# Operand pieces of the last layer in fixed slots, three queue orders changed, and the tail's splits one tile ahead

## The chip, the cores and the metric

The kernel runs on one core of a Trainium2 chip. The metric is the device time of one launch, in microseconds (us), as the median of several runs. TensorE (PE in the profile; PEld is its weight load) multiplies matrices into PSUM banks, VectorE (DVE) and ScalarE (ACT) work on tiles in SBUF and PSUM, GpSimd (POOL) works on SBUF tiles and issues indirect DMAs, and SyncE (SP) issues the other DMAs. Each engine takes its own instructions in program order and waits for semaphores of the others.

## The reference, cut to what matters

```python
x = attention(q, k, v)            # sliding window of 64, 4 x 8 heads, 576 positions of 64
x = moe(x, ...)                   # 2304 tokens, 8 experts, the best two of each token
g   = x @ w_gate                  # last layer: 2304 x 512 by 512 x 1536
val = x @ w_val                   # the same shape
out = (g * 1 / (1 + exp(-g)) * val) @ w_out     # 2304 x 1536 by 1536 x 512
```

All of it is float32. The change touches the last layer (`_moe2_ref`) and the end of the expert layer that feeds it.

## The kernel before, in words

**Precision.** A matrix operand is cut into two parts, hi and lo (`x = hi + lo`). ACT copies hi into an fp32r tile, DVE subtracts it from the original to get lo, and three products (hi-hi, hi-lo, lo-hi) are accumulated. So each operand costs one ACT copy and one DVE subtraction before TensorE may use it.

**The two wide products.** `g` and `val` are computed together as one 2x2 block product with seven block products instead of eight (Strassen-Winograd). Its operands are seven blocks of x (IA11, IA12, IS1 to IS4, IA22) and seven of the weights (IB11, IB21, IT1 to IT4, IB22); the S and T blocks are sums, made by DVE in place in the raw tile. `x_pieces(p)` makes the x blocks of one third p of the tokens (six tiles of 128), `w_pieces(k)` the weight blocks of one slice k of 128 columns. Raw weights are loaded by `load_w(k)` into one tile, `wr`, through SP's queue.

**A unit** is one pair (slice, third): seven block products of six 128x384 matmuls each (L1049). There are 36, in the order of the list `units`. `unit(n)` writes the program of unit n interleaved with the end of unit n-1: `first`, `second`, IS4 of n-1, IS2, IS3, IA22 of n-1, IS1. The products IA11, IS2, IS1 (and IS4 one unit later) go one after another into the same bank B. Between them `keep` copies the bank's running sum out on ACT (L1059); the next product into that bank must wait for that copy. `add` (L1066) adds bank A or D to a kept sum on DVE, `gate` takes the sigmoid on ACT (L1070), `times` multiplies on DVE or POOL (L1073), `store` writes the result u to DRAM through SP. The tile S1 of the kept sum has one buffer, S2 and S4 have two.

**The queue of pieces.** Everything that is not part of a unit (splits, sums, loads, gathers, combining of expert outputs) stands in a list `todo2`. `other()` pops one entry; it is called seven times in a unit and five times in a product of the third kind. The list `plan` says at which unit which entries are appended; an entry then gets whatever call comes next.

**The third product.** `third(T)` multiplies tile T of u (128 tokens) by w_out: 36 matmuls of 128x512 (L1176). `load_u(T)` reads the tile back, `u_pieces(T)` splits it in two halves (L1161 on ACT, L1162 on DVE) into one of two buffers. From unit 26 on one `third` follows each unit; the eight tiles 10 to 17 come after the last unit, back to back. They are "the tail" below. The result of each tile is copied from its bank to one buffer, by ACT for even and DVE for odd tiles, and scattered to its rows by POOL.

**Before the first unit** the last expert's five second products (`mm2`, L278) run. Between them `last_mm2(t)` gathers the expert outputs of the tokens (`early_y`, POOL), weighs them (`weigh`: ACT L729, DVE L730), transposes them on TensorE (`trans_c`, L195, copied out by ACT L742), and starts the x and w pieces.

Of the kernel before, what the change touches and what calls it, by code (L numbers as in the profile page):

```python
# [53 lines left out]
def tile_attention_moe_swiglu(ctx: ExitStack, tc: tile.TileContext, qh, kh, vh, wgn, noise, w1h, w2h,  # L54
# [655 lines left out]

    def other(k=1):
        for _ in range(k):
            if todo2:
                todo2.pop(0)()
# [29 lines left out]
    def x_pieces(p):  # L744
# [11 lines left out]
        def start():  # L756
            XS2[p] = pools[f"x{p}"].tile([128, 2, 7, 2, NB2], F32R, name=f"x{p}", tag=f"x{p}")
            hi(IA11, 0)
            sm(4, 2, ALU.add, 3)

        return [start,
                lambda: (hi(IA12, 1), lo(IA11, 0)),
                lambda: (hi(IS1, 4), lo(IA12, 1), sm(2, 0, ALU.subtract, 2)),
                lambda: (hi(IS3, 2), lo(IS1, 4), sm(4, 4, ALU.subtract, 0)),
                lambda: (hi(IS2, 4), lo(IS3, 2)),
                lambda: (hi(IA22, 3), lo(IS2, 4), sm(4, 1, ALU.subtract, 4)),
# [5 lines left out]
    def load_w(k):  # L772
        WR[k] = w = pools["rw"].tile([128, 7, 2, 128], F32, name=f"wr{k}", tag="wr")
# [4 lines left out]
    def w_pieces(k):  # L778
        def sums():
            WS2[k] = pools["rw" if k % 3 < 2 else "x2"].tile([128, 2, 7, 2, 128], F32R, name=f"ws{k}",  # L780
                                                             tag=f"ws{k % 3}")
            w = WR[k]
            for o, a, b in ((IT1, IT3, IB11), (IT2, IB22, IT1), (IT3, IB22, IT3), (IT4, IB21, IT2)):
                nc.vector.tensor_tensor(w[:, o], w[:, a], w[:, b], op=ALU.subtract)  # L784
# [118 lines left out]
    if True:  # L903
# [24 lines left out]
        def last_mm1(f):  # L928
# [6 lines left out]
            if f == 7:  # L935
# [6 lines left out]
                todo2.extend(x_pieces(0))  # L942

        def last_mm2(t):
            if t == 0:
                nc.scalar.preload_act_table_set("sigmoid_and_others")
                other(5)
            if t == 1:
                other(3)
                scopes["p2"].close()  # L950
                pools["x1"] = pool("x1", "right")
                weigh(6)
                weigh(7)
            if t == 2:
                trans_c(6)
                trans_c(7)
                weigh(8)
                todo2.extend(w_pieces(0))
                other(3)
                load_w(1)  # L960
                early_y(9)
                early_y(10)
            if t == 3:
                trans_c(8)
                early_y(11)
                weigh(9)
                weigh(10)
            if t == 4:
                trans_c(9)
                trans_c(10)  # L970
                weigh(11)
# [61 lines left out]
    for fs in ((0, 1, 2), (3,), (4,), (5,), (6,), (7,), (8,), (9,), (10, 11)):  # L1033
# [47 lines left out]
    def unit(n):  # L1081

        now, old = n < NU, n > 0
# [6 lines left out]
        other()  # L1090
        if now:
            second(n)
            add(n, A_[n], S1)
        other()
        if old:
            prod(B_[m], m, IS4, IB22, False, True)
        if now:
            gate(n, 0, S1)
        if old:
            times(m, 0, B_[m])  # L1100
            store(m, 0)
        other()
# [4 lines left out]
        other()  # L1107
# [3 lines left out]
        other()  # L1111
# [3 lines left out]
        other()  # L1115
# [3 lines left out]
        if old:  # L1119
            gate(m, 1, S2)  # L1120
            times(m, 1, S2[m])
            times(m, 1, S4[m], nc.gpsimd if now else nc.vector)
            store(m, 1)
        other()
# [4 lines left out]

    def o_load(j):  # L1130
        if j == 0:
            OW["a"] = pools["x0"].tile([128, 2, 10, 512], F32R, name="ow", tag="x0")
            r = rx.tile([128, 3584], F32, name="ur", tag="xr")
# [225 lines left out]
```

## Time and profile before

| | us |
|---|---|
| median of 3 runs | 1055.04 (1054.79 to 1057.38) |
| the profiled execution's own time | 1062.48 |
| its span, first to last instruction | 1060.7 |
| TensorE busy | 991.2 (93%) |
| VectorE busy | 683.8 (64%) |
| ScalarE busy | 432.3 (41%) |
| GpSimd busy | 227.3 (21%) |

The profiled execution lies 7.4 us above the median; 1.8 us of its time lie outside the span. Busy times are summed over a core's whole span, over stages that are limited by different things, so the stages have to be looked at one by one.

### The profile page before, as it was taken

What the parts mean: (1) busy time and instruction counts of PE and PEld (TensorE: products, weight loads), DVE (VectorE), ACT (ScalarE), POOL (GpSimd) and SP (SyncE); (2) the same over time, 40 slices, a digit from 0 to 9 for tenths busy, and PEclk for the clock granted to TensorE, in tenths of its full rate; (3) what the DMA queues carried; (4) which work ended last, traced back from release to release, by engine and by line L of the source; (5) the groups of instructions that cost most, each with busy time, mean ns of one, the idle gap of its engine ahead of it and who ended that gap; (6) DMA issues with size and microseconds to landing.
All of it is one profiled execution on the core that took longest, in us unless ns stands there. A gap on an engine that the chain in (4) does not pass through costs nothing.

```text
span 1060.7 us, 17386 instructions
## 1 busy us (share of the span) xinstructions
PE 991.2 (93%) x6538; PEld 875.5 (83%) x6538; DVE 683.8 (64%) x1318; ACT 432.3 (41%) x952; POOL 227.3 (21%) x301
## 2 busy tenths in 40 slices
PE   7978999999999999999999897899998999999886
PEld 5756888889898898989897797889997889988664
DVE  5797836868786877878256666687667665653211
ACT  6867334414242333324255543554445333432210
POOL 2693025123111010010053051011124111111100
PEclk9989999999999999999999998999999999999999
DMA  7884136657685767666254254223356334443320
GB/s 227 293 266 121 38 118 211 198 192 219 187 242 184 222 189 220 201 202 210 71 148 149 88 145 130 59 66 86 99 150 177 112 119 142 139 121 110 104 96 32
DMA packets 115009, 161.31 MB, mean 152 GB/s; under 512 B 15383, under 2 KB 77975, under 8 KB 114919
## 3 DMA queue, kind: packets, MB, share of 16 engines
q1 hardware_dynamic: 101799, 126.79, 39.6%
q0 software_dynamic: 7936, 23.91, 7.5%
q10 hardware_dynamic: 5184, 9.44, 2.4%
q8 instruction: 53, 0.87, 0.3%
q14 instruction: 37, 0.30, 0.1%
HBM read 117.07 MB, written 43.04 MB: 151 GB/s over the span
## 4 chain that ended last, share of the span: by engine, by line
PE 68%; DVE 14%; issue 6%; DMA 5%; ACT 5%; SPq 0%; ACTq 0%; POOL 0%; DVEq 0%
PE y L278 19%; PE h L256 16%; PE o L1176 13%; PE b L1049 8%; PE d L1049 4%; DVE wr L784 2%; PE a L1049 2%; DMA wr<-w_d 2%; PE sc L419 1%; PE gt L236 1%; ACT ws L787 1%; DVE s L1066 1%; ACT u L1070 1%; DMA k<-in_k_dram 1%; DVE nm L429 1%
## 5 line engine op out<-in xcount | busy, mean ns | idle before, releaser
L278 PE MATMUL y<-wp,ht 128*128 128x512 f32 (+6 forms) x960 | 228.7, 394 | 0.0
L256 PE MATMUL h<-xh,wp 128*128 128x256 f32 (+6 forms) x1536 | 221.5, 304 | 4.1 <-DVE ht L261 2.7
L256 PEld LDWEIGHTS h<-xh,wp 128*128 128x128 f32 x1536 | 215.7, 189 | 8.4 <-DVE ht L261 5.0
L278 PEld LDWEIGHTS y<-wp,ht 128*128 128x128 f32 (+6 forms) x960 | 172.5, 183 | 40.6
L1049 PE MATMUL b<-x,ws 128*128 128x384 f32 x864 | 171.4, 345 | 18.4 <-ACT s L1059 18.2
L1049 PEld LDWEIGHTS b<-x,ws 128*128 128x128 f32 x864 | 154.5, 192 | 25.3 <-ACT s L1059 24.5
L1176 PE MATMUL o<-ow,ou 128*128 128x512 f32 x540 | 129.7, 395 | 11.9 <-DVE ou L1162 6.2
L1176 PEld LDWEIGHTS o<-ow,ou 128*128 128x128 f32 x540 | 101.8, 190 | 36.5 <-DVE ou L1162 8.8
L221 POOL DMA_INDIRECT xg<-x_d,idx_i x38 | 36.8, 967 | 287.7 <-PE gt L236 241.2
L258 ACT ACTIVATE ht<-h 128x256 fp32r<-128x256 f32 (+7 forms) x128 | 53.1, 422 | 108.0 <-PE h L256 87.3
L1059 ACT ACTIVATE s<-b 128x384 f32<-128x384 f32 x108 | 52.4, 485 | 92.3 <-PE b L1049 89.4
L1073 POOL TENSOR_TENSOR u<-s,u 128x384 f32<-128x384 f32 x35 | 37.1, 1061 | 241.3 <-DVE u L1073 204.3
L283 ACT ACTIVATE ys<-y 128x512 f32<-128x512 f32 (+6 forms) x40 | 23.8, 596 | 159.5 <-PE y L278 137.0
L1049 PE MATMUL d<-x,ws 128*128 128x384 f32 x432 | 81.9, 337 | 0.4 <-DVE s L1066 0.4
L127 DVE TENSOR_TENSOR wp<-raw,wp 128x1024 fp32r<-128x1024 f32 x55 | 67.4, 1226 | 21.7 <-ACT wp L126 16.2
L1049 PEld LDWEIGHTS d<-x,ws 128*128 128x128 f32 x432 | 75.6, 188 | 1.0 <-DVE s L1066 1.0
L261 DVE SCALAR_TENSOR_TENSOR ht<-h,ht 128x256 fp32r<-128x256 f32 (+7 forms) x128 | 59.3, 467 | 19.5 <-ACT ht L258 17.8
L241 DVE TENSOR_TENSOR xh<-gt,xh 128x512 fp32r<-128x512 f32 (+6 forms) x40 | 25.7, 662 | 68.7 <-ACT xh L238 62.4
L1162 DVE TENSOR_TENSOR ou<-ur,ou 128x768 fp32r<-128x768 f32 x36 | 33.6, 953 | 55.9 <-ACT ou L1161 55.9
L1073 DVE TENSOR_TENSOR u<-s,u 128x384 f32<-128x384 f32 x73 | 42.9, 588 | 40.2 <-ACT u L1070 40.0
L787 ACT ACTIVATE ws<-wr 128x1024 fp32r<-128x1024 f32 (+1 forms) x48 | 44.4, 945 | 59.2 <-DVE wr L784 59.2
L126 ACT ACTIVATE wp<-raw 128x1024 fp32r<-128x1024 f32 x55 | 58.1, 1056 | 17.0 <-DMA raw<-in_w_dram 12.7
(206 smaller groups left out, 1342.7 us busy)
## 6 DMA issues: line engine op xcount, KB each, us to landing
raw<-in_w_dram SPq DMA_DIRECT2D x64, 512.0 KB
u_d<-u SPq DMA_DIRECT2D x72, 192.0 KB
ur<-u_d SPq DMA_DIRECT2D x18, 768.0 KB
wr<-w_d SPq DMA_DIRECT2D x48, 256.0 KB
w_d<-da ACTq DMA_DIRECT2D x36, 256.0 KB
y_d<-ys SPq DMA_DIRECT2D x34, 256.0 KB
rd<-in_wg_dram SPq DMA_DIRECT2D x12, 512.0 KB
rd<-in_wv_dram SPq DMA_DIRECT2D x12, 512.0 KB
```

Source lines behind the costliest of these rows:

```text
L126: nc.scalar.activation(w[:, 0, :], r, AF.Copy)
L127: nc.vector.tensor_tensor(w[:, 1, :], r, w[:, 0, :].bitcast(F32), op=ALU.subtract)
L221: nc.gpsimd.indirect_dma_start(out=g[0:m, :], out_offset=None, in_=x_d[0:rows, :], in_offset=bass.IndirectOffsetOnAxis(ap=idx(t)[0:m, :], ...
L256: nc.tensor.matmul(b_, w[:, a, k, fc], xh[:, c, k, 0:m], start=(n == 0), stop=(n == 11))
L258: nc.scalar.activation(ht[:, 0, f, 0:m], b_, AF.Relu)
L261: nc.vector.scalar_tensor_tensor(ht[:, 1, f, 0:m], b_, 0.0, ht[:, 0, f, 0:m].bitcast(F32), op0=ALU.max, op1=ALU.subtract)
L278: nc.tensor.matmul(b_, ht[:, a, f, sl], w[:, c, f % 2, :], start=(f == 0 and n == 0), stop=(f == 7 and n == 2))
L787: nc.scalar.activation(WS2[k][:, 0, a:b], WR[k][:, a:b], AF.Copy)
L1049: nc.tensor.matmul(b_, w[:, a, wi, k, :], x[:, c, xi, k, :], start=(start and i == 0), stop=(stop and i == 5), skip_group_check=True)
L1059: nc.scalar.activation(to[n], B_[n], AF.Copy)
L1073: eng.tensor_tensor(UT[n, h], v, UT[n, h], op=ALU.mult)
L1176: nc.tensor.matmul(ob, u[:, a, f, :], w[:, c, :], start=(f == 0 and n == 0), stop=(f == 11 and n == 2))
```

## The change: what it does

1. `todo2` holds pairs (slot number, entry). `slot_()` replaces `other()` in the units and the third products: it runs the entries whose number has come, and counts on. The numbers are written out (`put`, `w_put`); the list `plan` is gone.
2. `x_pieces` has eleven entries instead of eight and `w_pieces` five instead of three: the ACT copy and the DVE subtraction of one block stand in different entries.
3. In `unit`, `gate(n, 0)` is queued on ACT behind `keep(n, 2)` instead of ahead of it. `times(n, 0, S1)` stands one product later. The multiplications and the store of the second half of unit m (`times(m, 1, ...)`, `store(m, 1)`) stand in unit m+2 instead of at the end of unit m+1.
4. Raw weights of slices 4 and 5 are loaded into the place of the raw x tile (`xw`), those of slice 13 into a part of the tile for w_out.
5. At the end of the expert layer: the table load of the sigmoid set stands before the last expert's second products instead of behind the first of them; the gathers of tiles 9 to 11 get a tile of their own and stand behind the second of these products; the transposes of tiles 9 to 11 all stand behind the fourth; x pieces of the second third and the pieces of slice 1 stand there too.
6. In the list of units the slices 9, 10 and 11 form one group instead of (9) and (10, 11).
7. The splits of w_out are spread over units 22 to 26; two of the six subtractions are on POOL instead of four. `load_u(T + 2)` is issued at the end of the split of tile T. In the tail the split of tile T+1 stands inside `third(T)`.

```diff
     def other(k=1):
         for _ in range(k):
             if todo2:
-                todo2.pop(0)()
+                todo2.pop(0)[1]()
+    def slot_():
+        while todo2 and todo2[0][0] <= now_[0]:
+            other()
+        now_[0] += 1
...
-        def split(a, b):
+        def hi(a, b):
             nc.scalar.activation(WS2[k][:, 0, a:b], WR[k][:, a:b], AF.Copy)
+        def lo(a, b):
             nc.vector.tensor_tensor(WS2[k][:, 1, a:b], WR[k][:, a:b], WS2[k][:, 0, a:b].bitcast(F32), op=ALU.subtract)
-        return [sums, lambda: split(0, 4), lambda: split(4, 7)]
+        return [lambda: sums((IT1, IT3, IB11), (IT2, IB22, IT1)),
+                lambda: sums((IT3, IB22, IT3), (IT4, IB21, IT2)),
+                lambda: (place(), hi(0, 4)),
+                lambda: (hi(4, 7), lo(0, 4)),
+                lambda: lo(4, 7)]
...
             if t == 1:
...
+                for T in range(9, 12):
+                    early_y(T)
...
             if t == 3:
+                for T in range(9, 12):
+                    trans_c(T)
+                xq[:], wq = x_pieces(1), w_pieces(1)
+                todo2.extend((-1, o) for o in xq[:5] + wq[:2] + xq[5:6] + wq[2:])
...
+        if n > 1:
+            times(n - 2, 1, S2[n - 2])
+            times(n - 2, 1, S4[n - 2], nc.gpsimd if now else nc.vector)
+            store(n - 2, 1)
...
             prod(B_[m], m, IS4, IB22, False, True)
-        if now:
-            gate(n, 0, S1)
...
             prod(B_[n], n, IS2, IT2, False, False)
             keep(n, 2, S2)
-            times(n, 0, S1[n])
+            gate(n, 0, S1)
...
             if b == 12:
                 ready.add(("t", T))
+                if T < NT - 2:
+                    load_u(T + 2)
...
-        plan[last[k - 3] + 2] += w_pieces(k) + [lambda k=k: k + 1 < 24 and load_w(k + 1)]
+    put(2, (2,), [lambda: (w_raw(4), w_raw(5))])
+    w_put(5, 6, (4, 6, 7, 9, 10))
+        w_put(k, 2 * k - 4, (3, 4, 6, 7, 10), k + 1)
...
+    for T in range(12, NT):
+        todo2.extend((at(37, 5 * (T - 12) + s), o) for s, o in zip((0, 2), u_pieces(T)))
...
     for T in range(NU + 1 - 26, NT):
         third(T)
-        if T + 2 < NT:
-            load_u(T + 2)
-        if T + 1 < NT:
-            todo2.extend(u_pieces(T + 1))
```

The first place is ScalarE's queue in unit 7. `s_7` from `b` are the copies `keep`, `u_0` and `u_1` the sigmoids, `ws` the hi copies of a weight slice (slice 5 here). Before:

```order
474 L1059 ACTIVATE s_7_7207<-b_7200 128x384
475 L787 ACTIVATE ws_7210<-wr_7177 128x1024
476 L1070 ACTIVATE u_0_7231<-s_7_7207 128x384
477 L787 ACTIVATE ws_7210<-wr_7177 128x768
478 L1059 ACTIVATE s_7_7243<-b_7200 128x384
```

After, with the same names (`gl` is a gathered tile that is weighed):

```order
470 L1085 ACTIVATE s_7_7211<-b_7204 128x384
471 L801 ACTIVATE ws_7214<-xw 128x1024
472 L801 ACTIVATE ws_7214<-xw 128x768
473 L1085 ACTIVATE s_7_7243<-b_7204 128x384
474 L1096 ACTIVATE u_0_7245<-s_7_7211 128x384
475 L738 ACTIVATE gl<-gl,recp 128x512
```

The second copy of bank b stands ahead of the sigmoid now, and the weights come from the tile `xw`.

The second place is SP's queue of DMAs around the loads of slices 4 and 5 (from `w_d_81` and `w_d_82`); `u_d` are the stores. Before the change the queue reads:

```order
300 L1078 DMA u_d<-u_1_7117 128x3x128
301 L1078 DMA u_d<-u_0_7075 128x3x128
302 L776 DMA wr_7177<-w_d_81 128x4x128
303 L776 DMA wr_7177<-w_d_82 128x4x128
304 L1078 DMA u_d<-u_1_7195 128x3x128
```

After the change the same loads stand further ahead in the program (behind unit 1's first store):

```order
291 L1104 DMA u_d<-u_0_6805 128x3x128
292 L788 DMA xw<-w_d_81 128x4x128
293 L788 DMA xw<-w_d_82 128x4x128
294 L788 DMA xw<-w_d_81 128x4x128
295 L788 DMA xw<-w_d_82 128x4x128
296 L1104 DMA u_d<-u_1_6913 128x3x128
```

Before, slice 5 was loaded behind the store of the second half of unit 4 and the first half of unit 5; now slices 4 and 5 stand together, ahead of the store of unit 1's second half.

The third place is ScalarE's queue where the tail begins. `ur<-o` is the copy of an even tile's result, `ou` two to four halves of splits. Before:

```order
693 L1161 ACTIVATE ou<-ur 128x768 x2
694 L1070 ACTIVATE u_1_9842<-s_35_9751 128x384
695 L1181 ACTIVATE ur<-o_9847 128x512
696 L1161 ACTIVATE ou<-ur 128x768 x4
697 L1181 ACTIVATE ur<-o_9937 128x512
```

After the change the queue reads, from the split of tile 10 on:

```order
700 L1193 ACTIVATE ou<-ur 128x768 x2
701 L1096 ACTIVATE u_1_9842<-s_35_9746 128x384
702 L1193 ACTIVATE ou<-ur 128x768 x2
703 L1215 ACTIVATE ur<-o_9847 128x512
704 L1193 ACTIVATE ou<-ur 128x768 x4
705 L1215 ACTIVATE ur<-o_9937 128x512
```

Two more halves (the split of tile 11) stand ahead of the copy of tile 10's result.

## Rows read from the trace of the kernel before

**Rows 1.** The page's first part: busy us (share of the span) xinstructions.

```profile
PE 991.2 (93%) x6538; PEld 875.5 (83%) x6538; DVE 683.8 (64%) x1318; ACT 432.3 (41%) x952; POOL 227.3 (21%) x301
```

**Rows 2.** TensorE's waits from 589 to 821.4: us in total, times, longest.

```profile
PE b L1049 <- ACT s L1059: 18.2, 16, 4.1
PE ct L195 <- DVE gl L730: 3.2, 4, 1.6
```

**Rows 3.** TensorE's waits from 554 to 589.1.

```profile
PE ct L195 <- DVE gm L730: 2.2, 1, 2.2
PE ct L195 <- issue: 2.0, 1, 2.0
```

**Rows 4.** TensorE's waits from 969 to the end.

```profile
PE o L1176 <- DVE ou L1162: 6.2, 7, 1.4
PE o L1176 <- ACT ou L1161: 5.7, 4, 1.4
```

**Rows 5.** Windows by stage: length, busy us (x) of each engine, PEclk, DMA.

```profile
589.00:614.10 25.10, 22.00 (x111) 20.07 (x109) 21.20 (x32) 14.60 (x24) 3.91 (x3) 0.93 0.23 61
614.10:821.40 207.30, 188.61 (x1039) 182.38 (x1040) 144.98 (x241) 96.03 (x171) 45.71 (x39) 0.98 0.41 115
821.40:971.40 150.00, 149.80 (x751) 135.40 (x750) 86.91 (x135) 55.55 (x90) 21.53 (x31) 1.00 0.40 122
971.40:1053.80 82.40, 70.45 (x289) 54.52 (x288) 17.16 (x22) 13.16 (x19) 8.70 (x13) 0.98 0.27 88
```

**Rows 6.** Timeline of PE: the second product of units 3 and 5.

```profile
616.35 1.20 PE L1049 MATMUL a<-x,ws 128*128 128x384 f32 x6
...
630.98 1.22 PE L1049 MATMUL a<-x,ws 128*128 128x384 f32 x6
```

**Rows 7.** Pieces of the chain that ended last: start us, us, what.

```profile
821.48 8.16 PE o L1176 x36
...
975.17 4.77 DMA ur<-u_d
```

**Rows 8.** Timeline of all engines in unit 7: start, us, engine [idle before <-releaser].

```profile
646.85 2.52 SPq L776 DMA_DIRECT2D wr<-w_d  x2
...
652.49 1.56 DVE L784 TENSOR_TENSOR wr<-wr 128x256 f32<-128x256 f32 x4 [3.58 <-DMA wr<-w_d]
...
655.86 0.47 ACT L1059 ACTIVATE s<-b 128x384 f32<-128x384 f32 x1
...
656.38 1.01 PE L1049 MATMUL b<-x,ws 128*128 128x384 f32 x2 [4.15 <-ACT s L1059]
```

**Rows 9.** Window just behind that wait, columns as in rows 5.

```profile
656.30:662.00 5.70, 5.62 (x18) 5.34 (x18) 3.24 (x7) 2.03 (x5) 1.01 (x1) 0.56 0.44 127
```

**Rows 10.** Groups by form, DVE and ACT, from 589 to 980: busy, mean ns.

```profile
L1066 DVE TENSOR_TENSOR s<-d,s 128x384 f32<-128x384 f32 x72 | 39.7, 551 | 19.8 <-PE d L1049 19.6
L788 DVE TENSOR_TENSOR ws<-wr,ws 128x1024 fp32r<-128x1024 f32 x23 | 28.2, 1225 | 11.3 <-ACT ws L787 11.3
L788 DVE TENSOR_TENSOR ws<-wr,ws 128x768 fp32r<-128x768 f32 x23 | 21.8, 950 | 0.2 <-ACT ws L787 0.2
L747 ACT ACTIVATE x<-xr 128x768 fp32r<-128x768 f32 x14 | 11.4, 839 | 7.6 <-DVE xr L754 7.5
L787 ACT ACTIVATE ws<-wr 128x1024 fp32r<-128x1024 f32 x23 | 24.4, 1061 | 57.3 <-DVE wr L784 57.3
```

**Rows 11.** Timelines of ACT and POOL before the first unit.

```profile
559.92 0.60 ACT L283 ACTIVATE ys<-y 128x512 f32<-128x512 f32 x1 [4.89 <-issue]
560.53 1.28 ACT L946 ACT_TABLE_LOAD   x1
...
573.67 0.94 POOL L724 DMA_INDIRECT gm<-y_d,slot_e  x1 [11.83 <-PE ct L195]
```

**Rows 12.** Timelines of POOL and DVE in unit 23.

```profile
787.71 2.49 POOL L1147 TENSOR_TENSOR ow<-ur,ow 128x1024 fp32r<-128x1024 f32 x1 [0.87 <-ACT ow L1146]
...
789.00 1.61 DVE L1073 TENSOR_TENSOR u<-s,u 128x384 f32<-128x384 f32 x1
```

More of the change, by code (lines that the diff above doesn't have):

```diff
@@ L1081, in unit @@
     def unit(n):
-        now, old = n < NU, n > 0
+        now, old = n < NU, 0 < n <= NU
         m = n - 1
@@ L1105, in unit @@
             keep(n, 2, S2)
-            times(n, 0, S1[n])
-        other()
+            gate(n, 0, S1)
+        slot_()
         if now:
@@ L1110, in unit @@
             prod(D_[n], n, IS3, IT3, True, False)
-        other()
+        slot_()
+        if now:
+            times(n, 0, S1[n])
         if old:
@@ L1114, in unit @@
             add(m, D_[m], S2)
-        other()
+        slot_()
         if now:
@@ L1177, in third @@
             if f in (1, 3, 5, 7, 9):
-                other()
+                slot_()
         ot = OW["o"]
@@ L1224, in tile_attention_moe_swiglu @@
-    tiles = iter(range(NT))
-    def tile_next():
-        T = next(tiles)
-        need(("t", T))
-        third(T)
-        if T + 2 < NT:
-            load_u(T + 2)
-        if T + 1 < NT:
-            todo2.extend(u_pieces(T + 1))
-    for n in range(NU + 1):
-        if n <= 26:
-            todo2 += plan[n]
-        unit(n)
-        if n >= 26:
-            todo2 += wq if n == 26 else plan[n]
-            tile_next()
-    for T in range(NU + 1 - 26, NT):
-        todo2[:0] = [nothing]
-        tile_next()
@@ L1245, in tile_attention_moe_swiglu, with at, put, w_put @@
-    while todo2:
-        other()
+    def at(n, slot):
+        return 7 * min(n, 26) + 12 * max(n - 26, 0) + slot
+    def put(n, slots, pieces):
+        assert len(slots) == len(pieces)
+        todo2.extend((at(n, s), o) for s, o in zip(slots, pieces))
+    def w_put(k, n, slots, nxt=None, place=None):
+        ps = w_pieces(k)
+        if nxt:
+            last_ = ps.pop()
+            ps.append(lambda: (last_(), load_w(nxt, place and place())))
+        put(n, slots, ps)
+    raw = {}
+    def w_raw(k):
+        if not raw:
+            raw[0] = rx.tile([128, 3840], F32, name="xw", tag="xr")
+        load_w(k, raw[0][:, 1792 * (k - 4):1792 * (k - 3)])
@@ new lines, in tile_attention_moe_swiglu @@
+    put(0, (0, 3), xq[0:2])
+    w_put(2, 0, (4, 6, 7, 10, 11), 3)
+    put(1, (0, 6, 8), xq[2:5])
+    put(2, (2,), [lambda: (w_raw(4), w_raw(5))])
+    for T in range(12, 18):
+        put(T - 11, (5,), [lambda T=T: late_y(T)])
+    w_put(3, 4, (3, 4, 6, 7, 10), 6)
+    w_put(4, 5, (4, 6, 7, 9, 10))
+    w_put(5, 6, (4, 6, 7, 9, 10))
+    for k in range(6, 11):
+        w_put(k, 2 * k - 4, (3, 4, 6, 7, 10), k + 1)
+    w_put(11, 18, (3, 4, 6, 7, 10), 12)
+    for T, a, b in ((12, (7, 4), (8, 0)), (13, (7, 6), (8, 2)), (14, (9, 2), (9, 6)), (15, (9, 4), (10, 0)),
+                    (16, (10, 0), (11, 0)), (17, (10, 2), (11, 2))):
+        put(a[0], a[1:], [lambda T=T: weigh(T)])
+        put(b[0], b[1:], [lambda T=T: trans_c(T)])
@@ new lines, in tile_attention_moe_swiglu @@
+    for n in range(26, 36):
+        put(n, (2, 4), u_pieces(n - 26))
+        if n < 35:
+            w_put(n - 11, n, (7, 8, 9, 10, 11), n - 10 if n < 34 else None)
+    put(36, (2, 4, 7, 9), u_pieces(10) + u_pieces(11))
+    for T in range(12, NT):
+        todo2.extend((at(37, 5 * (T - 12) + s), o) for s, o in zip((0, 2), u_pieces(T)))
+    todo2.sort(key=lambda o: o[0])
+    for n in range(NU + 2):
+        unit(n)
+        if n == NU:
+            unit(n + 1)
+            third(n - 26)
+            break
+        if n >= 26:
+            third(n - 26)
@@ L1247, in tile_attention_moe_swiglu @@
+    for T in range(NU + 1 - 26, NT):
+        third(T)
+    assert not todo2
     for name in ("x2", "rs", "x1", "rw", "x0", "rx"):
```

151 lines of the change are left out of this document (72 added, 79 removed).

## Prediction

> **What bounds the kernel now.** I read the page first: TensorE is busy 93% of the span, the next engine 64% [rows 1]. So TensorE sets the time, and the question is where its time is more than its work. Then its waits by stretch, its timeline for the pace without waits, and a window for each stage. What to see: the pace of a unit is (630.98 - 616.35) / 2 = 7.32 us, or 1.045 for one of its seven products [rows 6], and a third product takes 8.16 [rows 7]. Against these, the stages stand so:
>
> - Before the first unit (554 to 589): waits of 2.2 and 2.0 [rows 3].
> - Units 0 to 2 (589.0 to 614.1): 18 products are 18.8 us of work in 25.1, so 6.3 are lost; 3.1 of it are idle (25.1 - 22.0), the rest is slow pace at a clock of 0.93 [rows 5].
> - Units 3 to 26 (614.1 to 821.4): 24 units and one product, 176.7, and six transposed tiles, put by estimate at a third of a product each, 2; so 28.6 of the 207.3 are lost, 18.7 idle [rows 5].
> - Units 27 to 36 with a third product each: TensorE is busy 149.8 of 150.0 [rows 5]. Nothing to win.
> - The tail: 8 x 8.16 = 65.3 of work in 82.4, so 17.1 are lost; its waits are 6.2 and 5.7 [rows 4, 5].
>
> In the second and third stages nearly all waits are for the copy of bank B (18.2 of 21.4, sixteen of them [rows 2]). Unit 7 shows how one comes about [rows 8]. SP issues the raw weights at 646.85 and DVE, which waits for them 3.58 us, starts the sums only at 652.49. Behind the sums on DVE stands the addition to S1, behind that addition on ACT the sigmoid, and behind the sigmoid the copy of bank B, which starts at 655.86. TensorE stood idle 4.15 us, though neither sums nor sigmoid concern its next product. After such a wait the granted clock is 0.56, near the lower of its two levels (1.2 GHz), for some microseconds: 18 matmuls took 5.7 us, at the pace above 3.1 [rows 9]. The long waits thus cost about half as much again as they show.
>
> **The change, part by part.** The sum is made against the profiled execution: 1062.48 us, of which 1060.7 are span. It lies 7.4 above the median, and the trace does not show where those come from; I take the saving off the median unchanged, and the upper end of the range allows for some of the 7.4 lying in waits that go away.
>
> Before the first unit. The table load (1.28) moves into ACT's idle 4.89, ahead of the first y copy [rows 11], so the x pieces start earlier; nothing waits for it, and without that cover it would cost its 1.28. The gathers of tiles 9 to 11, which waited 11.83 us on POOL for a transposed tile to leave its place [rows 11], now wait for the second y product only. The last transpose stands ahead of the fifth y product, which covers its copy. I keep about 1 us: three transposes share two banks, so the third of them waits for an ACT copy, twice. Saving 4.2 - 1.0 = 3.2; bounds 1 and 4.2.
>
> Units 0 to 2. ACT now gets four copies of pieces between the fifth y copy and the first `keep`: two of x at 0.84, one of w at 1.06, one of the 768 width, 0.84 by the x row [rows 10]. With the y copy's 0.60 [rows 11] that is 4.2 us, and the third product of unit 0 wants its copy 2 x 1.045 = 2.1 after the start: a wait of 2.1, plus about 0.5 for the copy itself. The raw weights of slice 2 share one tile with slice 1 and are asked for only behind its last split, and the multiplication that frees S1 (one buffer) is queued behind their sums on DVE: about 1 more. So 3.6 of the 6.3 remain: saving 2.7, say 2.5; bounds 0 (these waits also lower the clock, as now) and 5.
>
> Units 3 to 26. (a) The copy ahead of the sigmoid cuts the chain of unit 7 at its last link; nothing on TensorE waits for a sigmoid soon. (b) Slices 4 and 5 are in place three units before use; the 3.58 goes. (c) Later slices are loaded one unit, 7.32, before their sums; the load of unit 7 took 652.49 - 646.85 = 5.64 from issue to use [rows 8], so 1.7 us to spare. If one comes late, DVE's sums hold up the sigmoid of the second half and the weights' own copies, and the next unit's first copy behind those. (d) DVE in a unit with a slice: six of its own operations at 0.55, four sums 1.56, two subtractions 1.23 and 0.95 [rows 8, 10]: 7.0 of 7.32. It fits, with nothing to spare; but DVE need not keep time with each product, only stay within a few products. Over the stage DVE has 145 us of work [rows 5] for about 181. (e) The second half's multiplications stand a unit later; `keep` of the next sum into the same S2 buffer now waits for one of them. DVE is done with it about 1.6 us into the unit (0.47 for the copy before it, 0.55 for an addition, 0.55 for itself; 3.9 where an ACT copy of 1.06 and a subtraction of 1.23 of weights stand ahead); the copy can't start before four products, 4.2. Hidden, by 0.3 at worst. Behind it on ACT stands the sigmoid, which nobody waits for soon, and TensorE has two more products, 2.1, before it needs the copy. For S4 it is the same with POOL's multiplication, about 1 us, and three products more in between. (f) w_out: ACT's copies are the same; DVE takes two subtractions more, POOL two fewer. In unit 22 two of them and the sums of slice 12 meet: 3.3 + 2 x 1.23 + 1.56 = 7.3, so the next unit's first copy comes just late, some tenths of a us.
> Left over: I take 3.6 of the 28.6, for (c), (d), (f) and restarts. Saving 25; bounds 17 (a third stays) and 28.
>
> Units 27 to 36: the pieces keep their places within a unit; 0, bounds -2 and 0.
>
> The tail. Each third product now starts when its tile's split has been done during the one before. The split was queued behind the copy of the previous result, so TensorE waited for both; moved ahead by one tile it has 8.16 us of cover. The load of tile T+2 goes out at the end of the split of tile T, some 13 us before its own split; one took 4.77 [rows 7]. The result's one buffer is refilled every 8.16 instead of every 10.3. At the head two multiplications more stand ahead of the split of tile 10 on DVE: -1. Saving 17.1 - 1.1 = 16; bounds 12 and 17.
>
> Sum: 3.2 + 2.5 + 25 + 0 + 16 = 46.7. Median 1055.0 - 46.7 = 1008.3, so **1008 us**. All lower bounds together (28) would give 1027, all upper ones (54.2) 1001.
>
> **The rivals.**
>
> *GpSimd takes time from DVE in the dense units.* A DVE operation that met POOL's subtraction of w_out took 1.61 us instead of 0.55: it started at 789.00 and ended at 790.61, just behind POOL's end at 790.20 [rows 10, 12]. If each two-input SBUF operation of DVE has to wait for POOL's, units 23 and 24, where POOL has a w_out subtraction (about 2.5) and a multiplication (about 1), have 7.0 + 3.5 = 10.5 us of DVE time for 7.32: 3.2 lost in each, 6.4. In the other dozen units with a slice POOL's 1 us makes 8 of 7.3: up to 0.7 each, 8 in all if none of it can be made up in the unit between. So 1008 + 6 to 14: 1015 to 1022. Against it: POOL's multiplication mostly meets DVE operations that read a bank, and the units without a slice give back. It decides if more than 0.3 us of a dense unit is blocked.
> The Trainium skill, "SBUF — State Buffer", section "SBUF: two separate sides", says this as a rule: the ports that DVE and GpSimd share are an exclusive lock, also for a DVE operation with two SBUF inputs against a GpSimd one that reads SBUF. By that rule the trace's 1.61 is a full wait, which fits to 0.2 us (790.20 and 0.55 make 790.75, it ended at 790.61), and this change is worth 33 to 40 us instead of 47.
>
> *The tail gains nothing.* If the operand of tile T+2 or the result's buffer came late, the period would stay at 10.3: 1008 + 16 = 1024. Against it: 4.77 in 13 us. It decides if loads take over 13 us.
>
> *The slots change the order, not the time.* A slot is a place in the program; ACT may still reach the bank's copy late, behind weight copies that wait for DVE. Then half of units 3 to 26 stays: 1008 + 12 = 1020. For it: sixteen waits in units that are not alike. Against it: in unit 7 the late things were a load and a sigmoid, both moved.
>
> *Slower than before.* The one new wait on TensorE's chain is (e): `keep` behind a multiplication of the same unit. If DVE came to it 4.2 + 2.1 = 6.3 us into the unit or later, each microsecond beyond would be lost 36 times; 46.7 are used up at 1.3 a unit, that is, when DVE runs 7.6 us behind TensorE, a whole unit, in steady state. With 7.0 of work in 7.32 in the dense units and 3.3 in the others it does not build up. Time then: over 1055.
>
> **How the numbers follow.** The forecast 0.60 (1001 to 1015), GpSimd 0.18, order without time 0.10, the tail 0.05, better than the upper bounds 0.04 (below 1001), slower 0.03. The likeliest gives 1008. The range 1000 to 1022 takes in the forecast, most of GpSimd's and of the third rival's. A measurement of this kernel tells 0.3%, 3.2 us, from no change. Every case but the last is faster by far more: faster 0.95, same 0.02 (several losses together), slower 0.03.
>
> **What would show it.** In the trace after: waits for the bank's copy from unit 3 to 26 below 4 us in all, the stage about 182 long, none above 2, the clock at 1.00 there; third products of the tail 8.2 apart with no waits for `ou`; DVE's sums without a wait for `wr`; the first unit's start 3 us earlier. Wrong it would be if the sums still wait for DMAs, if DVE operations of 0.55 show 1.5 in many units, if the copy into S2 follows a DVE release in steady state, or if the tail's period stays above 9.

## The result and the profile after

The changed kernel takes 1011.81 us (median of 4 runs, 1010.88 to 1013.43) where the kernel before takes 1054.91 beside it (1053.14 to 1057.38). The ratio is 0.9591, with a 95% interval of 0.9568 to 0.9615. The prediction was 1008. The profiled execution took 1010.88 us, with a span of 1009.1 and a mean granted clock of 0.992.

The page's first part, which answers to [rows 1]: TensorE has gone from 93% of the span to 97%, with 16.5 us less busy time for the same number of instructions.

```profile
PE 974.7 (97%) x6538; PEld 871.5 (86%) x6538; DVE 674.9 (67%) x1321; ACT 430.8 (43%) x952; POOL 224.2 (22%) x298
```

TensorE's waits from 545 us to the end (us in total, times, longest), which answer to [rows 2 to 4]:

```profile
PE b L1075 <- ACT s L1085: 6.8, 5, 2.6
PE o L1210 <- DVE ou L1194: 0.8, 1, 0.8
PE ct L195 <- ACT xr L751: 0.6, 2, 0.3
PE d L1075 <- DVE s L1092: 0.2, 1, 0.2
```

The sixteen waits for the copy of bank B in [rows 2] were 18.2 us. Three of the five that are left stand in units 23 to 25, 2.1 us together; the other two stand in units 0 and 1. The waits for late transposes (3.2) are gone, and of the tail's 11.9 there is 0.8 left.

The windows of the stages, with the columns of [rows 5], from the first y product of the last expert on: before the first unit, units 0 to 2, 3 to 26, 27 to 36, the tail.

```profile
546.40:577.50 31.10, 30.50 (x147) 23.92 (x146) 22.78 (x30) 21.69 (x32) 14.63 (x12) 1.00 0.57 169
577.50:603.20 25.70, 20.99 (x109) 20.31 (x109) 18.06 (x30) 11.61 (x20) 6.24 (x5) 0.93 0.33 88
603.20:785.60 182.40, 180.28 (x1040) 179.13 (x1040) 139.66 (x238) 93.01 (x171) 39.63 (x35) 1.00 0.43 122
785.60:935.70 150.10, 149.90 (x752) 135.53 (x751) 81.66 (x138) 56.20 (x90) 19.66 (x29) 1.00 0.41 128
935.70:1002.30 66.60, 65.76 (x289) 53.81 (x287) 18.12 (x23) 13.87 (x19) 8.71 (x13) 1.00 0.34 112
```

Against before (34.85, 25.1, 207.2, 150.1 and 82.4), measured between the same instructions, the stages gained 3.7, -0.5, 24.8, 0 and 15.7 us: 43.7 in all, where the medians differ by 43.1. The forecast was 3.2, 2.5, 25, 0 and 16. So one term came out on the wrong side of nothing: units 0 to 2. The profiled execution of before reached the first y product at 554.15 and this one at 546.43, in products that the change doesn't touch. Before's 7.4 us above its median most likely lie there, since the stages behind it repeat from trace to trace (the next section); so it was right to take the saving off the median.

The timeline of all engines from unit 0 to unit 1 (start, us, engine, in brackets the idle time before and its releaser; `wr` is the one raw tile, `ws` a split slice, `x` a split set of activations):

```profile
578.24 1.57 ACT L756 ACTIVATE x<-xr 128x768 fp32r<-128x768 f32 x2
579.71 1.78 ACT L801 ACTIVATE ws<-wr 128x1024 fp32r<-128x1024 f32 x2
581.39 0.47 ACT L1085 ACTIVATE s<-b 128x384 f32<-128x384 f32 x1
581.91 1.31 PE L1075 MATMUL b<-x,ws 128*128 128x384 f32 x6 [2.09 <-ACT s L1085]
582.90 1.22 SPq L788 DMA_DIRECT2D wr<-w_d  x2
...
589.06 0.89 DVE L794 TENSOR_TENSOR wr<-wr 128x256 f32<-128x256 f32 x2 [3.97 <-DMA wr<-w_d]
589.86 0.55 DVE L1099 TENSOR_TENSOR u<-s,u 128x384 f32<-128x384 f32 x1
...
590.50 0.49 ACT L1085 ACTIVATE s<-b 128x384 f32<-128x384 f32 x1 [4.67 <-DVE u L1099]
...
591.05 2.22 PE L1075 MATMUL b<-x,ws 128*128 128x384 f32 x6 [2.62 <-ACT s L1085]
```

The first wait is the one forecast, behind four copies ahead of the first `keep`. The second is the chain that the prediction put at "about 1": the raw weights of slice 2 are asked for at 582.90, their sums start at 589.06, the multiplication that frees S1 stands behind those sums, and the copy into S1 behind that. TensorE stood 2.62 us. Then it ran for some 3 us at the low clock, as the window just behind the wait shows (granted clock 0.53, near the lower level of 1.2 GHz; 0.79 in the 2.5 us after it):

```profile
591.00:593.50 2.50, 2.45 (x8) 2.46 (x9) 2.50 (x6) 1.14 (x2) 0.00 (x0) 0.53 0.00 0
```

### The profile page after: what moved, and what is told of

It is laid out like the page before. It is cut to its first block, busy times and chain, and to the rows that moved or that the text cites. A ratio compares the mean times of both kernels' runs of the same rounds, so it can differ in the third digit from the quotient of the medians.

```text
span 1009.1 us, 17409 instructions
## 1 busy us (share of the span) xinstructions
PE 974.7 (97%) x6538; PEld 871.5 (86%) x6538; DVE 674.9 (67%) x1321; ACT 430.8 (43%) x952; POOL 224.2 (22%) x298
## 5 line engine op out<-in xcount | busy, mean ns | idle before, releaser
L1075 PE MATMUL b<-x,ws 128*128 128x384 f32 x864 | 167.1, 339 | 6.8 <-ACT s L1085 6.8
L1210 PE MATMUL o<-ow,ou 128*128 128x512 f32 x540 | 125.7, 390 | 0.8 <-DVE ou L1194 0.8
L1099 POOL TENSOR_TENSOR u<-s,u 128x384 f32<-128x384 f32 x34 | 34.7, 1020 | 154.6 <-DVE u L1099 115.2
L804 DVE TENSOR_TENSOR ws<-wr,ws 128x1024 fp32r<-128x1024 f32 (+1 forms) x42 | 46.1, 1121 | 19.4 <-ACT ws L801 19.4
L1222 POOL DMA_INDIRECT out_dram<-ur,recp x17 | 18.4, 1080 | 182.8 <-DVE ur L1217 89.0
L432 ACT ACTIVATE att<-sc,nms 128x128 f32<-128x128 f32 x144 | 50.5, 379 | 15.9 <-DVE nms L430 14.8
```

What stands on the lines that cost most here:

```text
L432: nc.scalar.activation(p[:, h2, hp, :], scb[T][h2][:, hp, :], AF.Exp, bias=nms[:, h2, hp:hp + 1], scale=0.125, accum_out=rs[:, h2, hp:hp + 1])
L1075: nc.tensor.matmul(b_, w[:, a, wi, k, :], x[:, c, xi, k, :], start=(start and i == 0), stop=(stop and i == 5), skip_group_check=True)
L1210: nc.tensor.matmul(ob, u[:, a, f, :], w[:, c, :], start=(f == 0 and n == 0), stop=(f == 11 and n == 2))
```

## The experiments

All twelve runs are profiled, and outside the stage that an edit touches their stages repeat to about 0.1 us. The exception is units 0 to 2, told below. So the table gives stage lengths from the traces, between the starts of the same instructions: the first y product, the first product of unit 0, the products into bank a of units 3, 27 and 35, and the end of the last third product. Units 0 to 2 so counted hold 20 products, 20.9 us at the pace of [rows 6]; units 3 to 26 include the first third product. Units 27 to 34 so counted were 123.86 in every run. The time up to the first y product went from 546.4 to 554.2 from profile to profile, and that noise is in the ratios.

| kernel | median us | ratio to before (95%) | before first unit | units 0-2 | units 3-26 | from unit 35 |
|---|---|---|---|---|---|---|
| before | 1054.91 | 1 | 34.85 | 27.35 | 214.17 | 99.38 |
| changed | 1011.81 | 0.9591 (0.9568-0.9615) | 31.12 | 27.76 | 189.49 | 83.65 |
| a1 sigmoid first | 1013.94 | 0.9563 (0.9534-0.9591) | 31.12 | 26.06 | 189.87 | 83.61 |
| b1 copy first, in before | 1057.44 | 0.9984 (0.9964-1.0004) | 34.81 | 27.24 | 212.48 | 99.37 |
| a2 raw in turn | 1026.97 | 0.9689 (0.9653-0.9725) | 31.12 | 26.97 | 199.30 | 83.58 |
| s2 units 3-21 in a row | 1020.79 | 0.9655 (0.9618-0.9693) | 31.18 | 27.25 | 195.48 | 83.61 |
| s3 w_out as before | 1021.06 | 0.9659 (0.9628-0.9689) | 31.12 | 27.61 | 199.06 | 83.61 |
| a3 tail in turn | 1032.77 | 0.976 (0.9719-0.9801) | 31.16 | 25.42 | 189.45 | 98.85 |
| g1 four on GpSimd | 1014.98 | 0.9635 (0.9598-0.9672) | 31.12 | 27.28 | 190.83 | 83.61 |
| d1 splits in unit 25 | 1014.74 | 0.9609 (0.9573-0.9645) | 31.12 | 27.19 | 190.44 | 83.61 |
| u1 sums behind | 1010.69 | 0.9572 (0.9537-0.9607) | 31.11 | 25.05 | 189.49 | 83.65 |
| u2 raw 2 early | 1009.66 | 0.9561 (0.9531-0.9592) | 31.11 | 23.31 | 189.48 | 83.61 |
| u3 u2 and copies moved | 1010.24 | 0.9567 (0.9533-0.9601) | 31.11 | 24.06 | 189.50 | 83.60 |
| m1 all mended | 1006.54 | 0.9533 (0.9507-0.956) | 31.12 | 21.33 | 190.46 | 82.45 |

The runs stood beside the kernel before on chips where its median was 1060.07 (a1, a2, a3, b1), 1055.88 (u2, u3, s2, s3) and 1056.38 (m1, d1, g1, u1).

### What made the 25 us of units 3 to 26

Theory: the three things that held up the copy of bank B (a late load, pieces in a row, the crowded w_out stage) each carry a part. Rival: the copy ahead of the sigmoid alone carries most of it.

**a1**, the order of copy and sigmoid undone:

```diff
-            keep(n, 2, S2)
             gate(n, 0, S1)
+            keep(n, 2, S2)
```

> The changed kernel with one step taken back: the sigmoid of the first half stands ahead of the copy of the bank again. The prediction did not divide its 25 us of units 3 to 26 between copy order, raw weights and slots. If the order of copy and sigmoid carries most of it, half of the waits return: 1011.8 + 8 to 14, 1020 to 1026, with waits for the copy of the bank in many units. If the slots and the early raw weights carry it, the sigmoid is hardly ever late: in the changed kernel it waited for DVE five times, 7.6 us in all, all in the units behind 690 us, and the copy has about 2 us to spare each time. Then 1011.8 + 2 to 5, 1014 to 1017, and new waits only in units 22 to 25.

Units 3 to 26 took 189.87, 0.4 longer. What ACT waited for there, in this run:

```profile
ACT u L1096 <- DVE s L1092: 24.7, 21, 2.4
```

And TensorE there:

```profile
PE b L1075 <- ACT s L1085: 1.8, 3, 0.8
```

The sigmoid, now ahead, waits for DVE 21 times, 24.7 us in all (6.8, 4 times, in the changed kernel), and TensorE hardly notices (2.1, 3 times, in the changed kernel): the copy has time to spare when nothing else is late.

**b1**, that step alone, in the kernel before:

```diff
-        if now:
-            gate(n, 0, S1)
...
             keep(n, 2, S2)
+            gate(n, 0, S1)
             times(n, 0, S1[n])
```

> The kernel before with one step of the change alone: the copy of the bank for the second sum ahead of the sigmoid, everything else as before. If the order of copy and sigmoid carries most of the gain of units 3 to 26, 1054.9 - 10 to 14, 1041 to 1045. If not, because the hi copies of the weights, which wait for the late sums, still stand ahead of the copy on ACT, 1054.9 - 0 to 5, 1050 to 1055, and the sixteen waits for the copy of the bank (18.2 us) are still most of what TensorE waits for.

Units 3 to 26 gained 1.7. Unit 7 of this run, the place of [rows 8]:

```profile
649.92 1.55 DVE L784 TENSOR_TENSOR wr<-wr 128x256 f32<-128x256 f32 x4 [3.21 <-DMA wr<-w_d]
651.17 1.79 ACT L787 ACTIVATE ws<-wr 128x1024 fp32r<-128x1024 f32 x2 [5.14 <-DVE wr L784]
...
652.87 0.47 ACT L1059 ACTIVATE s<-b 128x384 f32<-128x384 f32 x1
...
653.39 2.35 PE L1049 MATMUL b<-x,ws 128*128 128x384 f32 x12 [3.38 <-ACT s L1059]
```

The sigmoid is out of the way, and the copy stands behind the two hi copies of the slice, which wait for the same late sums: 3.38 instead of 4.15. Both runs say that the order alone is worth little, 0.4 us where it is taken out of the change and 1.7 where it is put into the kernel before; the rival falls.

**a2**, slices 4 and 5 through the one raw tile again:

```diff
-    put(2, (2,), [lambda: (w_raw(4), w_raw(5))])
-    w_put(3, 4, (3, 4, 6, 7, 10), 6)
-    w_put(4, 5, (4, 6, 7, 9, 10))
-    w_put(5, 6, (4, 6, 7, 9, 10))
...
+    w_put(3, 4, (3, 4, 6, 7, 10), 4)
+    w_put(4, 5, (4, 6, 7, 9, 10), 5)
+    w_put(5, 6, (4, 6, 7, 9, 10), 6)
```

> The changed kernel, but the raw weights of slices 4 and 5 go through the one raw tile in turn, each asked for behind the last split of the slice before. If late raw weights are a cause on their own, DVE stands some 5 us in unit 5 and in unit 6, TensorE waits 2 to 4 us in each or in the next, and each wait is followed by a stretch at the low clock: 1011.8 + 6 to 12, 1018 to 1024. If the copy ahead of the sigmoid is enough to cover a late load, 1012 to 1014.

9.8 us of the 25 are back. The timeline around both slices, and the window behind the first wait:

```profile
637.84 0.89 DVE L794 TENSOR_TENSOR wr<-wr 128x256 f32<-128x256 f32 x2 [6.46 <-DMA wr<-w_d]
640.65 2.29 PE L1075 MATMUL b<-x,ws 128*128 128x384 f32 x6 [4.39 <-ACT s L1085]
650.28 0.89 DVE L794 TENSOR_TENSOR wr<-wr 128x256 f32<-128x256 f32 x2 [5.93 <-DMA wr<-w_d]
653.09 1.31 PE L1075 MATMUL b<-x,ws 128*128 128x384 f32 x6 [2.72 <-ACT s L1085]
```

```profile
640.60:644.00 3.40, 3.35 (x10) 3.36 (x11) 3.40 (x6) 2.58 (x4) 2.46 (x2) 0.50 0.20 55
```

Two waits of 7.1 together cost 9.8; the rest is mostly the low clock behind the first of them (behind the second the granted clock was 1.00, from 653.0 to 656.0). The copy ahead of the sigmoid, which this kernel has, did not cover the late loads.

**s2**, the pieces of units 3 to 21 in the places of the kernel before (slices 3 to 11 one unit later in a row, transposes in units 8 and 10, the third set of x in units 12 and 14 with its old grouping):

```diff
-    w_put(3, 4, (3, 4, 6, 7, 10), 6)
+    w_put(3, 5, (0, 0, 1, 1, 2), 6)
...
-        w_put(k, 2 * k - 4, (3, 4, 6, 7, 10), k + 1)
+        w_put(k, 2 * k - 3, (0, 0, 1, 1, 2), k + 1)
...
-    put(11, (4, 6, 7, 9, 18, 20, 21, 23, 32, 34, 35), x_pieces(2))
+    put(12, range(4), xq[:4])
+    put(14, range(4), xq[4:])
...
```

> The changed kernel with the pieces of units 3 to 21 back in the places of the kernel before: weight pieces in a row at the head of a unit, transposes and x pieces in a row in units 8, 10, 12 and 14; the early raw weights, the copy ahead of the sigmoid and the w_out stage stay as changed. The kernel before idled 3.2 us there for transposes, 3.7 in the x pieces and about 1 elsewhere. If the slots are what removed these, they return with about half as much again of low clock: the changed kernel's time + 8 to 13. If the copy ahead of the sigmoid covers them, + 0 to 3.

6.0 us are back, a little under the expected 8. Four waits for transposes return (`gl L739`, 2.9 us in all) and one for the copy behind the x pieces (1.26, at 702.60). The window of the whole stage, with the columns of [rows 5]:

```profile
608.50:804.00 195.50, 189.15 (x1070) 184.31 (x1070) 149.54 (x247) 98.29 (x175) 40.20 (x35) 1.00 0.42 121
```

The five waits are 4.1 of the 6.0. The rest is no low clock, for it was 1.00 throughout: TensorE's busy time is 1.8 longer (187.38 between the same instructions of the changed kernel), in part because a product behind a wait has none before it to overlap and a first matmul of 0.44 us instead of 0.33 (at 702.60). In the units that have weight pieces alone no wait returns; what shows is that a transpose's operand has to be weighed well ahead, and x pieces spread.

**s3**, the w_out stage as before (four of six splits on GpSimd, slices 12 to 14 one unit later):

```diff
-    put(22, (0, 2), [o_split(0), o_split(1)])
-    w_put(12, 22, (3, 4, 6, 7, 10), 14)
+    put(23, (0, 1, 3), [o_split(0), o_split(1, nc.gpsimd), o_split(2)])
+    w_put(12, 23, (4, 4, 5, 5, 6), 14)
...
+    put(24, (5, 6, 7), [o_split(3, nc.gpsimd), o_split(4, nc.gpsimd), lambda: load_u(0)])
...
+    put(25, (5, 6), [o_split(5, nc.gpsimd), lambda: load_u(1)])
```

> The changed kernel with the splits of w_out in units 23 to 25 (four of six on GpSimd) and the pieces of slices 12 to 14 one unit later, as in the kernel before. That kernel idled 5.7 us in units 23 to 25. If the places and the engines of these pieces are what the change mended, the time of the changed kernel + 6 to 9, with a wait above 3 behind a DVE operation that ran beside GpSimd's subtraction. If the early raw weights of w_out and the copy order are enough, + 0 to 3.

9.6 us are back, by two waits. The timeline at both:

```profile
762.61 1.06 ACT L1179 ACTIVATE ow<-ur 128x1024 fp32r<-128x1024 f32 x1 [1.93 <-DMA ur<-w_d]
763.69 1.23 DVE L1180 TENSOR_TENSOR ow<-ur,ow 128x1024 fp32r<-128x1024 f32 x1 [3.11 <-ACT ow L1179]
764.84 1.55 DVE L794 TENSOR_TENSOR wr<-wr 128x256 f32<-128x256 f32 x4
767.19 0.65 PE L1075 MATMUL b<-x,ws 128*128 128x384 f32 x2 [4.48 <-ACT ws L801]
...
780.48 2.40 POOL L1180 TENSOR_TENSOR ow<-ur,ow 128x1024 fp32r<-128x1024 f32 x1 [0.57 <-ACT ow L1179]
781.29 3.71 DVE L794 TENSOR_TENSOR wr<-wr 128x256 f32<-128x256 f32 x4
...
786.91 3.23 PE L1075 MATMUL b<-x,ws 128*128 128x384 f32 x12 [2.21 <-ACT s L1085]
```

In unit 23 a split waits for its raw piece of w_out, and slice 12, whose sums stand behind that split on DVE, comes too late for its first product. In unit 25 the four sums take 3.71 instead of 1.55 beside GpSimd's subtraction. The early raw weights alone don't carry this stage.

9.8 + 6.0 + 9.6 = 25.4, where the whole is 24.7 by this count: undone one at a time, the three parts add up to a little more than all of it. b1, which has the order of copy and sigmoid and none of the three, is 23.0 longer than the changed kernel in this stage. So the three carry 23.0 together, some of it counted twice in the 25.4, and the order the 1.7 that is left. The regrouping of slices 9 to 11 and the later place of the second half's multiplications were undone in no run.

### GpSimd beside DVE

Theory: GpSimd's subtraction holds DVE up, but DVE's slack hides most of it. Rival (of the prediction): it costs its length.

**g1** puts splits 0 and 1 on GpSimd too:

```diff
-    put(22, (0, 2), [o_split(0), o_split(1)])
+    put(22, (0, 2), [o_split(0, nc.gpsimd), o_split(1, nc.gpsimd)])
```

> The changed kernel with four splits of w_out on GpSimd instead of two (the two of unit 22 too), in the same places. If GpSimd's subtraction blocks DVE for its length (the prediction's rival), each of the two costs up to 2.5 of DVE's time in a unit that is full and gives it back 1.23: the changed kernel's time + 1 to 4, and DVE operations of 0.55 to 1.23 stretched beside it. If DVE is mostly free to go on, DVE has 2.5 less to do: - 1 to 0.

Timeline of POOL and DVE in unit 22 of this run, and the product that waited:

```profile
748.94 2.40 POOL L1180 TENSOR_TENSOR ow<-ur,ow 128x1024 fp32r<-128x1024 f32 x1 [7.19 <-ACT ow L1179]
749.92 5.74 DVE L794 TENSOR_TENSOR wr<-wr 128x256 f32<-128x256 f32 x4
751.30 1.19 POOL L1099 TENSOR_TENSOR u<-s,u 128x384 f32<-128x384 f32 x1
752.46 2.57 POOL L1180 TENSOR_TENSOR ow<-ur,ow 128x1024 fp32r<-128x1024 f32 x1
...
758.52 1.72 PE L1075 MATMUL b<-x,ws 128*128 128x384 f32 x6 [1.79 <-ACT s L1085]
```

Four sums that take 1.55 alone took 5.74. Three of them ended 0.3 us behind one of POOL's three operations (751.62 behind 751.34, 752.78 behind 752.49, 755.32 behind 755.03), and the last took its usual 0.41. TensorE waited 1.79, where the changed kernel waits 0.43, so about a third of the 4.2 us of block reached it. The stage grew by 1.3, at the low end of what the rival gives. That is not more waiting: later waits became shorter, and all of them are 2.14 us, as in the changed kernel (2.12). It is mostly the clock, granted at 0.65 and 0.67 in the two stretches of 2.5 us behind the 1.79. The Trainium skill, "SBUF — State Buffer", section "SBUF: two separate sides", calls the ports that the two engines share an exclusive lock; the trace agrees, a DVE operation with two SBUF inputs waits out POOL's.

**d1** takes all of w_out off GpSimd:

```diff
-    put(23, (1,), [o_split(2, nc.gpsimd)])
...
-    put(24, (1, 3), [o_split(3, nc.gpsimd), lambda: load_u(0)])
...
-    put(25, (4,), [o_split(4)])
+    put(24, (3,), [lambda: load_u(0)])
+    put(25, (0, 1, 6), [o_split(2), o_split(3), o_split(4)])
```

> The changed kernel, but GpSimd splits no w_out: splits 2 to 4 are all on DVE in unit 25, which has no weight slice. If GpSimd's subtractions hold up DVE's operations on SBUF in units 23 and 24 (two sums took 3.08, two subtractions 4.48 beside them), the waits of 0.43, 0.60 and 1.09 in units 23 to 25 go: the changed kernel's time - 1.5 to 2.5. If DVE is simply full there, the wait moves to units 25 and 26: 0, or up to 1 more.

The stage grew by 0.95: the waits of 0.60 and 1.09 went, and four others came with units 25 and 26 (0.72, 0.52, 0.61, 0.16), where DVE is now full: the second of the two cases expected. It shows the other side of the block. In the changed kernel GpSimd's two subtractions cost DVE about 4.6 us of standing (two sums took 3.08 instead of 0.8, two subtractions 4.48 instead of 2.1) and spare it 2.5 of work, and spread over two units that is the better of the two ways tried.

### Units 0 to 2

Theory: the late load of slice 2's raw weights, with the multiplication for S1 behind its sums, stops TensorE in unit 1. Rivals: the load is late for another reason; the order on DVE is enough.

**u1** moves the first two sums one slot back, behind that multiplication:

```diff
-    w_put(2, 0, (4, 6, 7, 10, 11), 3)
+    w_put(2, 0, (5, 6, 7, 10, 11), 3)
```

> The changed kernel with the first two sums of slice 2 one slot later, behind the multiplication that frees the one buffer S1; the raw weights still come as late as before. If the order on DVE is what makes the late load stop TensorE in unit 1, the wait of 2.6 goes there, and the late slice costs at most about 1 at the first product of unit 2: the changed kernel's time - 2 to 4. If the late load stops TensorE anyway, - 1 to + 1, with a wait for `ws` or for a copy behind the hi copies.

The wait in unit 1 is gone, though the sums start as late as before (592.53, with 3.22 of waiting for the load asked for at 586.66). Units 0 to 2 took 25.05. The seven kernels that leave this stage as it is took 25.4 to 27.8, so it is the trace, not the length, that shows this.

**u2** gives slice 2 a place of its own, asked for when the last y product is done:

```diff
...
+    gl = ls.tile([128, 10752], F32, name="gl", tag="x2")
+    G["late"] = gl[:, 0:6144].rearrange("p (t c d) -> p t c d", t=6, c=2)
+    load_w(2, gl[:, 6144:7936])
+    load_w(3)
...
```

> The changed kernel, but the raw weights of slice 2 have a place of their own (behind the late gathered tiles in the place of the third set of pieces), asked for when the last y product is done, some 4.5 us earlier than behind slice 1's last split. If the late load is what stops TensorE in unit 1 (2.6 us, and a stretch at half clock behind it), both go: the changed kernel's time - 3 to 5, a ratio to the kernel before 0.003 to 0.005 smaller. If the load is late for another reason (it shares the DMA engines with the gathers, or its place comes free late), the sums still wait and nothing changes.

The load went out at 581.26, 3.99 ahead of the next load into `wr` (585.25); the sums didn't wait for it, and units 0 to 2 took 23.31. Only the wait of 2.09 is left.

**u3** also moves three hi copies behind the first copy of the bank:

```diff
-                todo2.extend((-1, o) for o in xq[:5] + wq[:2] + xq[5:6] + wq[2:])
...
+                todo2.extend((-1, o) for o in xq[:5] + wq[:2])
...
-    put(0, (0, 3), xq[0:2])
...
+    put(0, (0, 1, 2, 2, 3, 3, 4), xq[0:3] + [lambda: load_w(3)] + xq[3:6])
...
```

> As the run with slice 2's raw weights in a place of their own, and the two hi copies of slice 1 and one of x are moved from ahead of the first copy of the bank into the slots of unit 0. If the wait of 2.09 in unit 0 is these copies, as the prediction put it, it goes too: units 0 to 2 take 19 to 21 us instead of 25.7, the changed kernel's time - 5 to 7. If the moved copies now stand ahead of later copies of the bank, the wait moves within unit 0 or to the first product of unit 1 (slice 1 late): - 3 to - 4, no better than the run with the place alone.

Units 0 to 2 took 24.06, no better. The timeline of its first copy (the lines of this kernel stand one lower):

```profile
581.93 0.49 ACT L1084 ACTIVATE s<-b 128x384 f32<-128x384 f32 x1 [2.48 <-DMA y_d<-ys]
...
582.47 1.31 PE L1074 MATMUL b<-x,ws 128*128 128x384 f32 x6 [1.54 <-ACT s L1084]
```

Behind the four copies stood a second cause at almost the same time: the buffer S1 lies where the rows `ys` lay, and the copy waits for their last store. A wait of 1.54 stays, and 0.99 comes back in unit 1, where DVE, which itself waited 2.46 for that copy and has a piece of x more to do in unit 0, is late with the sums.

**m1** mends both, and takes in d1 and a head for the tail:

```diff
-    rs, rx = pool("rs", "right"), pools["rx"]
+    rs, rx = pool("rs", "right", "tile"), pools["rx"]
...
+    put(0, (0, 1, 2, 2, 3, 4), xq[0:3] + [lambda: load_w(3)] + xq[3:5])
...
+        if n == 35:
+            put(n, (8, 10), u_pieces(10))
...
```

> The changed kernel with four things mended: slice 2's raw weights early in a place of their own; the hi copies of slice 1 behind the first copy of the bank, whose buffers wait tile by tile for what lay there before (that copy was found to wait for the last store of y rows); splits 2 to 4 of w_out on DVE in unit 25; the split of tile 10 one third product earlier. If each wait left is a loss of its own, the gains add up: about 3 for unit 1, 1.8 for unit 0, 2 for units 23 to 25 and 0.8 at the tail, 7 to 8 in all, a ratio to the kernel before of 0.951 to 0.953. If a mended wait only makes the next late thing show, as when the hi copies were moved, 3 to 4, a ratio of 0.955 to 0.957.

1006.54 us, a ratio of 0.9533 (0.9507 to 0.956), below the changed kernel's by intervals that don't meet. Its units 0 to 2 as a window, with the columns of [rows 5]:

```profile
581.90:601.50 19.60, 19.54 (x111) 19.17 (x111) 18.54 (x31) 10.89 (x19) 6.49 (x5) 1.00 0.40 115
```

TensorE is busy 19.54 of 19.6 at the full clock. From the first y product to the end of the last third product it gains 6.7 over the changed kernel: 6.4 in units 0 to 2 (5.7 against the mean of the seven kernels that leave them as they are), 1.2 at the tail, and d1's 1.0 lost, which is why it stays a little under the 7 to 8 expected. The same without d1 would be about 1 us better by this count; it was not run.

### The tail

**a3**, each split from tile 11 on behind the third product before it and its copy:

```diff
-    put(36, (2, 4, 7, 9), u_pieces(10) + u_pieces(11))
-    for T in range(12, NT):
-        todo2.extend((at(37, 5 * (T - 12) + s), o) for s, o in zip((0, 2), u_pieces(T)))
+    put(36, (2, 4), u_pieces(10))
+    for T in range(11, NT):
+        todo2.extend((at(37, 5 * (T - 11)), o) for o in u_pieces(T))
```

> The changed kernel, but each split of the tail from tile 11 on stands behind the third product of the tile before and its copy again, the loads as in the changed kernel. If the split one tile ahead is the whole of the tail's gain: a period of about 10.3 instead of 8.16 for seven tiles, 1011.8 + 13 to 16, 1025 to 1028, with waits of TensorE for `ou` of 1.2 to 1.4. If the earlier load had a part in it, less: 1016 to 1023, with the waits below 1.

The tail grew by 15.2 of the 15.7. TensorE's waits from 540 us on are those of [rows 4] again:

```profile
PE o L1210 <- DVE ou L1194: 7.1, 8, 1.4
PE o L1210 <- ACT ou L1193: 5.7, 4, 1.4
```

The place of the split is the whole gain; the earlier load has no part that shows. The run's ratio gives some 18 us, some 5 either way.

## Why the prediction was right, and where not

- **Before the first unit**: 3.7 measured, 3.2 forecast; the two waits behind transposes that share two banks are there, 0.30 each instead of the 1 us kept for both. No run divides the 3.7 among the table load, the gathers and the transposes.
- **Units 0 to 2: the step that failed.** Forecast +2.5, measured -0.5 in the profile. The term named both causes. The first was put at 2.1 and 0.5 for the copy, and was 2.09 in all; the second was put at "about 1 more". It was 2.62, and about 1.7 more went at the low clock behind it. The load was priced by its place in the program and not from its request: asked for at 582.90 and 5.64 from issue to use [rows 8], it couldn't be summed before 588.5, when the copy was wanted at 588.4; the sums and the multiplication behind them had to be added whole. u1 and u2 show both halves of that chain. In the seven kernels that leave this stage as changed it took 25.4 to 27.8 (mean 27.1), the first wait 2.09 or 2.12 in each and the second 0.34 to 2.62; the kernel before took 27.35 by this count, so the gain is 0.3 on the mean.
- **Units 3 to 26**: 24.8 forecast 25, the stage 182.4 forecast 182, the clock 1.00, waits of 2.1 in all, none above 1.1. TensorE idles 16.5 us less and is busy 8.1 less, by the clock (0.98 before) and, it seems, by fewer restarts; DVE's sums wait for no load there. The size was right. It was no sum of (a) to (f) but the loss less 3.6 that would stay, so it could come out with a wrong reason among them; (a) was wrong. The sigmoid was the last link of unit 7's chain, not its cause: alone its move gave 1.7, undone it cost 0.4. (b) gave 9.8, the slots of transposes and x pieces 6.0, the w_out stage, for which the prediction had no saving of its own and a small loss, 9.6. That waits cost about half as much again held as a size, 7.1 us for 9.8 (a2) and 4.1 for 6.0 (s2), but the low clock that the prediction gave as the reason stood behind one of these waits alone, the first of a2; in s2 it was 1.00 throughout.
- **(e)**, the copy into S2 behind a multiplication: ACT waited so twice in units 3 to 26, 2.0 us in all, hidden from TensorE.
- **The tail**: 15.7 forecast 16. Third products start every 8.16, and the one wait (0.84) is the loss of 1 foreseen at its head; m1 shows that it goes when the split of tile 10 stands one third product earlier.
- **Rivals.** GpSimd's block is real, and in one group of four sums larger (4.2 in g1) than the 3.5 us a unit of the rival, but in the changed kernel TensorE waits 1.1 at most in a unit of that stage, not 3.2. A slice is summed two units ahead of its use, which would explain it; no run tests that. Slots changed the time, not only the order (s2). The case of a slower kernel did not come.

## What to carry to other kernels

Before moving the last link of a chain of waits, ask when the next link would have let the work go: the saving is the difference, here 0.77 of 4.15 us. Price a load from the moment at which its request can leave (its place must be free), and add what stands behind its first user on that user's queue. When two things are late at nearly the same time, mending one moves the wait (u3); the trace names only the later of them.

## What the runs showed of the hardware

The same wait of 2.09 us in unit 0 was followed by a granted clock of 1.00 in the changed kernel's profile and of 0.54 in u1's, though TensorE's rows ahead of it are alike. The windows just behind it, of the changed kernel and of u1:

```profile
581.90:585.10 3.20, 3.19 (x18) 3.19 (x19) 3.18 (x5) 1.02 (x2) 2.36 (x2) 1.00 0.45 125
```

```profile
585.70:589.40 3.70, 3.70 (x12) 3.70 (x13) 3.60 (x6) 0.91 (x2) 2.32 (x2) 0.54 0.49 145
```

After one and the same wait the clock fell in one execution and not in the other. It was worth 1.6 us here (d's product took 2.04 instead of 1.20, b's 2.07 instead of 1.31), and is part of why units 0 to 2 don't repeat. Nor did the longer wait always lower it: behind the 4.15 us of unit 7 in the kernel before it was 0.56 [rows 9], behind the 3.38 us in the same place of b1 it was 1.00 (653.4 to 658.0). What decides it, these runs don't show.
